# Six of eight sums of squares as two single-pass products of split squares, in a fused attention and expert kernel

## The chip, the cores and the metric

One core of one Trainium2 chip. The metric is the device time of one execution in microseconds (us), the median of several. The engines are named as the profile names them: PE is TensorE (matmuls; PEld its weight loads), DVE is VectorE, ACT is ScalarE, POOL is GpSimd, and SP is SyncE, which here only issues DMAs.

## What is computed

Causal attention with a bias from running sums gives 2304 rows of 512. Each row goes to one of eight experts, then through RMS normalization and a gated layer:

```python
for e in range(E):
    mask = expert_idx == e
    xe = x[mask]
    h = np.maximum(xe @ w1[e], 0.0)
    ye = h @ w2[e]
    out[mask] = gate_w[mask, None] * ye
...
rms = np.sqrt(np.mean(x * x, axis=-1, keepdims=True) + 1e-06)
xn = x / rms * rms_g
g = xn @ w_gate
silu = g * (1.0 / (1.0 + np.exp(-g)))
return (silu * (xn @ w_val)) @ w_out
```

The change concerns the mean of x*x, taken over the 512 features of each row that leaves an expert.

## The kernel before

The program runs attention, then the experts one after another, then the gated layer. In PE, ACT, DVE and SP each stage's instructions stand in the order in which the Python code emits them; each engine works its own list in that order and waits on semaphores for the others.

An expert s holds n rows, n from 312 down to 248 for experts 1 to 7 (`CAP`). Features lie on the partitions and rows in the columns. `gemm1` makes eight tiles f of the hidden layer, 24 products to a pair of tiles: every operand is split into a high part (rounded to `float32r`) and a low part (the rest), and a product is three `float32r` products (`PASSES`). After a tile ACT takes Relu (L918, `h`, high part) and DVE makes the low part (L919). `gemm2` makes four tiles c of the output: ACT copies each to `y` (L940) and squares it (L945), and DVE adds the squares up in `sq` (L946), so that `sq` holds, on each of the 128 partitions, the sum over four of the 512 features.

`finish(s)` sums `sq` over the partitions by one product of a 128x128 matrix of ones with `sq`, in plain `float32` (L960, tile `ms`), takes the root on ACT (L962), the reciprocal on DVE (L963) and scales `y` (L966). It stands one expert late, behind tile f = 1 of the next expert's `gemm1`, so that `sq` has been ready for a while. The six places at which this happens for experts 1 to 6 are called handovers 1 to 6 below; handover 1 lies in expert 2, and so on.

The weights of a later expert are loaded in pieces of 512 KB to `raw` (SP, L732, four staging buffers). `split` makes their parts: ACT casts the high part (L747), and DVE takes the rest one call later (L760). One `split` stands behind each of the four tiles of `gemm2` (two behind c = 1) and three stand in `gemm1`. The one behind c = 3 stands just ahead of Relu f = 0 of the next expert in ACT's list.

Of the kernel before, what the change touches and what calls it, by code (L numbers as in the profile page):

```python
# [7 lines left out]
F32 = mybir.dt.float32  # L8
F32R = mybir.dt.float32r
# [3 lines left out]
ALU = mybir.AluOpType  # L13
# [6 lines left out]
E = 8  # L20
# [4 lines left out]
CAP = (312, 304, 300, 292, 284, 268, 248)  # L25
CM = CAP[0]
# [33 lines left out]
def consts(k):  # L60
    nc, P = k.nc, k.cpool
    k.ident = P.tile([128, 128], F32, name="ident")
    nc.gpsimd.memset(k.ident, 0.0)
    nc.gpsimd.affine_select(out=k.ident, in_=k.ident, compare_op=ALU.not_equal, fill=1.0, base=0,
                            pattern=[[-1, 128]], channel_multiplier=1)
    k.w8 = P.tile([128, E], F32, name="w8")
    nc.gpsimd.iota(k.w8, pattern=[[-1, E]], base=E, channel_multiplier=0, allow_small_or_imprecise_dtypes=True)
    k.tid = P.tile([128, 5], F32, name="tid")
    nc.gpsimd.iota(k.tid, pattern=[[128, 5]], base=0, channel_multiplier=1, allow_small_or_imprecise_dtypes=True)
    k.w8v = P.tile([128, 5, E], F32, name="w8v")  # L70
    nc.gpsimd.tensor_copy(k.w8v, k.w8.unsqueeze(1).broadcast_to((128, 5, E)))
    nc.gpsimd.memset(k.w8v[64:128, 4, :], 0.0)
    k.base = P.tile([128, E], F32, name="base")
    nc.gpsimd.iota(k.base, pattern=[[REG, E]], base=0, channel_multiplier=0, allow_small_or_imprecise_dtypes=True)
    k.ereg = P.tile([1, E], F32, name="ereg")
    nc.gpsimd.iota(k.ereg, pattern=[[REG, E]], base=0, channel_multiplier=0, allow_small_or_imprecise_dtypes=True)
    k.eid = P.tile([1, E], F32, name="eid")
    nc.gpsimd.iota(k.eid, pattern=[[1, E]], base=0, channel_multiplier=0, allow_small_or_imprecise_dtypes=True)
    cap = P.tile([1, E], F32, name="cap")
    k.cap, k.na = cap[:, 0:RANKS], cap[:, RANKS:E]  # L80
    for n, c in enumerate(CAP):
        nc.gpsimd.memset(k.cap[:, n:n + 1], float(c))
    k.ones32 = P.tile([128, 128], F32, name="ones32")
    nc.gpsimd.memset(k.ones32, 1.0)
    eps = P.tile([128, 6], F32, name="eps6")
    k.eps6, k.gv = eps[:, 0:1], eps[:, 2:6]
    nc.vector.memset(k.eps6, 1e-6)
    nc.scalar.activation(eps[:, 1:2], k.eps6, AF.Exp)
    k.nb = P.tile([1, NB], U32, name="nb")
    P.tile([128, 32], F32, name="space")  # L90
# [727 lines left out]
def tiles_of(n):  # L818
    return tuple((t, min(128, n - 128 * t)) for t in range((n + 127) // 128))
# [17 lines left out]
def load_late(k):  # L837
    k.xl = y_tile(k, "xl")[:, 0:XROW].unsqueeze(1)
    load_rows(k, k.xl, 0, LATE, slice(NA, NA + LATE))
# [10 lines left out]
def ids(k, x, tiles):  # L850
    nc = k.nc
    row = k.rpool.tile([1, CM], F32, name=f"ids{k.uid()}", tag="ids", bufs=1)
    ps = k.psum.tile([128, 512], F32, name=f"ip{k.uid()}", tag="b")
    n = 0
    for t, m in tiles:
        nc.tensor.transpose(ps[0:1, n:n + m], x[0:m, t, DM:DM + 1], k.ident[0:m, 0:m])
        n += m
    row = row[:, 0:n]
    nc.scalar.copy(row, ps[0:1, 0:n])
    return row  # L860


def keep_ids(k, row, column):
    n = row.shape[-1]
    k.nc.sync.dma_start(out=k.tokd[bass.ds(column, n)].unsqueeze(0), in_=row)
# [88 lines left out]
    return number(k, OFF + piece, NTOK)  # L954


def finish(k, s, n):
    nc = k.nc
    ps = k.psum.tile([128, 512], F32, name=f"ms{s}", tag="b")
    nc.tensor.matmul(ps[:, 0:n], k.ones32, k.sq[s][:, 0:n], start=True, stop=True)  # L960
    r = k.sq[s][:, 0:n]
    nc.scalar.activation(r, ps[:, 0:n], AF.Sqrt, bias=k.eps6, scale=1.0 / DM)  # L962
    nc.vector.reciprocal(r, r)  # L963
    y = k.y[s][:, :, 0:n]
    for c in range(4):
        nc.vector.scalar_tensor_tensor(y[:, c, :], y[:, c, :], k.gv[:, c:c + 1], r, op0=ALU.mult, op1=ALU.mult)  # L966
    return y
# [33 lines left out]
def turn_rows(k, y, out):  # L1001
    nc = k.nc
    ps = k.psum.tile([128, 512], F32, name=f"yt{k.uid()}", tag="b")
    for c in range(4):
        nc.tensor.transpose(ps[:, 128 * c:128 * c + 128], y[:, 128 * c:128 * c + 128], k.ident)
    nc.vector.tensor_tensor(out, ps.rearrange("p (c n) -> p c n", c=4),
                            k.gv.unsqueeze(2).broadcast_to((128, 4, 128)), op=ALU.mult)
# [5 lines left out]
def moe(k, close):  # L1013
    k.y, k.sq = {}, {}

    def rank(n):
        for _ in range(n):
            next(k.last, None)

    k.order = [(s, u, q) for s in range(1, E) for u in range(4) for q in (0, 2)]  # L1020
    words = [(E, 2, f) for f in range(4 + EARLY_OUT, NF)] + [(E, 0, 0), (E, 1, 0)]
    for n, item in enumerate(words):
        k.order.insert(WORDS_AT + 9 * n, item)
    chain = iter(())
    row = ids(k, k.x[0], EARLY)
    keep_ids(k, row, 0)
    rank(RANK[0])
    for f in range(8):
        gemm1(k, 0, f, NA)
        rank(RANK[f + 1])  # L1030
        if f == 3:
            load_late(k)
        if f in (2, 4):
            split(k, 1, False)
        elif f == 5:
            rest(k)
    load_x(k, 1)
    feed(k, STG - 1)
    first = tiles_of(CAP[0])
    gemm2(k, 0, 0, NA)  # L1040
    rank(1)
    gemm2(k, 0, 1, NA)
    rank(1)
    gate(k, k.xl, ((0, 128),))
    gemm2(k, 0, 2, NA)
    xb = [k.rpool.tile([128, 4, CP], F32R, name=f"xb{n}", tag=f"xt{n}", bufs=1)[:, :, 0:128] for n in range(2)]
    turn_tile(k, k.xl[:, 0, :], *xb)
    row = ids(k, k.xl, ((0, 128),))
    keep_ids(k, row, column(k, 1))
    split(k)  # L1050
    gate(k, k.x[1], first)
    split(k)
    gemm2(k, 0, 3, NA)
    split(k)
    k.hr = y_tile(k, "hr")[:, 0:1024]
    rows_gemm1(k, xb, 0)
    split(k)
    rows_gemm1(k, xb, 1)
    hb = [k.mpool.tile([128, 8, CP], F32R, name=f"hb{n}", tag=f"h{n}")[:, :, 0:128] for n in range(2)]
    turn_tile(k, k.hr[:, 0:512], *[t[:, 0:4] for t in hb])  # L1060
    x_transpose(k, 1, (0, 1), first)
    turn_tile(k, k.hr[:, 512:1024], *[t[:, 4:8] for t in hb])
    x_transpose(k, 1, (2, 3), first)
    split(k)
    y = finish(k, 0, NA)
    row = ids(k, k.x[1], first)
    yr = k.hr.rearrange("p (a n) -> p a n", a=2)
    k.yr = yr[:, 0, :]
    rows_gemm2(k, hb)
    keep(k, y, NA, 0)  # L1070
    keep_ids(k, row, column(k, 2))
    split(k)
    head = iter(())
    for s in range(1, E):
        last = s == E - 1
        n = CAP[s - 1]
        if last:
            rest(k)
            close()
            glu_first(k)  # L1080
            next(head)
        else:
            load_x(k, s + 1)
        for f in range(8):
            gemm1(k, s, f, n)
            if s == 1 and f == 0:
                y = yr[:, 1, :].rearrange("p (c n) -> p c n", c=4)
                turn_rows(k, k.yr, y)
            if s > 1 and f == 1:
                y = finish(k, s - 1, CAP[s - 2])  # L1090
            if f == 5:
                keep(k, y, CAP[s - 2] if s > 1 else LATE, column(k, s))
                if not last:
                    gate(k, k.x[s + 1], tiles_of(CAP[s]))
            if f in (1, 3, 5) or (s == 1 and f < 3):
                split(k)
            next(head, None)
        for c in range(4):
            gemm2(k, s, c, n)
            next(chain, None)  # L1100
            if c == 1:
                split(k)
            if not last:
                if c in (1, 2):
                    x_transpose(k, s + 1, (2 * c - 2, 2 * c - 1), tiles_of(CAP[s]))
                if c == 1:
                    row = ids(k, k.x[s + 1], tiles_of(CAP[s]))
                if c == 3:
                    keep_ids(k, row, column(k, s + 2))
            split(k)  # L1110
            if c == 0 and s <= len(words):
                chain = decode_words(k)
                next(chain)
            if s == E - 2 and c == 1:
                head = glu_head(k)
            next(head, None)
    assert not k.staged and not k.order

    def tail():
        keep(k, finish(k, E - 1, CAP[-1]), CAP[-1], column(k, E))  # L1120

    k.tail = tail
# [941 lines left out]
```

## Time and profile before

| what | value |
|---|---|
| median of 3 runs | 839.87 us (839.81 to 841.09) |
| the profiled execution's own time | 838.61 us |
| its span from first to last instruction | 836.9 us |
| PE busy | 816.7 us, 98% |
| PEld / DVE / ACT / POOL busy | 746.7 / 639.6 / 461.9 / 227.0 us |
| chain that ended last, PE's share | 92% |
| granted TensorE clock, mean | 0.994 |

The profiled execution is 1.3 us under the median of the runs, and 1.7 us of it lie outside the span. The experts 1 to 7 take from about 223 us to 416 us of the span.

### The profile page before, as it was taken

How to read it: one execution, taken by the hardware profiler on the slowest of the kernel's cores; microseconds unless marked ns; L12 is line 12 of the kernel's file. 1: busy time of each engine (PE TensorE's matmuls, PEld its weight loads, DVE VectorE, ACT ScalarE, POOL GpSimd, SP SyncE). 2: the span in 40 equal slices, each digit the busy share in tenths (PEclk: the TensorE clock that was granted, in tenths of full speed). 3: DMA queues.
4: the chain of work that ended last, by engine and by line, in shares of the span. 5: the costliest groups of instructions: out<-in, count | busy, mean ns of one | idle time of the engine just before them, and what ended most of it. 6: DMA issues, size and time to landing. Idle time of an engine off the chain costs nothing.

```text
span 836.9 us, 15788 instructions
## 1 busy us (share of the span) xinstructions
PE 816.7 (98%) x5622; PEld 746.7 (89%) x5622; DVE 639.6 (76%) x1425; ACT 461.9 (55%) x1060; POOL 227.0 (27%) x249
## 2 busy tenths in 40 slices
PE   7999999999999999999999999999999999999994
PEld 4777767789899999999999999999999998899994
DVE  6657688965866768777698988988888869868880
ACT  5988989865756656566543433333333334553440
POOL 3335856332000000000221233444343351031120
PEclk9999999999999999999999999999999999999997
DMA  7999989236567566767661332322222376344510
GB/s 226 299 320 314 315 245 295 84 126 214 193 193 245 179 228 204 237 206 233 225 197 66 131 109 103 131 94 98 104 100 99 108 282 191 81 151 146 159 52 29
DMA packets 79757, 146.72 MB, mean 175 GB/s; under 512 B 7424, under 2 KB 44315, under 8 KB 79667
## 3 DMA queue, kind: packets, MB, share of 16 engines
q1 hardware_dynamic: 76707, 136.08, 51.4%
q0 software_dynamic: 2912, 9.46, 3.0%
q8 instruction: 46, 0.75, 0.4%
q14 instruction: 44, 0.36, 0.1%
q10 hardware_dynamic: 48, 0.07, 0.0%
HBM read 108.04 MB, written 37.54 MB: 174 GB/s over the span
## 4 chain that ended last, share of the span: by engine, by line
PE 92%; DVE 3%; ACT 2%; DMA 1%; issue 1%; SPq 0%; POOL 0%; POOLq 0%; DVEq 0%; ACTq 0%
PE gg L1320 29%; PE g L938 12%; PE g L915 12%; PE gp L1778 10%; PE go L1713 6%; PE pvy L419 5%; PE t L373 5%; PE s L310 5%; PE tl L447 2%; PE sm L341 1%; PE xp L886 1%; ACT pt L406 1%; DMA ringa<-ytd 1%; PE r L987 1%; PE r L976 1%
## 5 line engine op out<-in xcount | busy, mean ns | idle before, releaser
L938 PE MATMUL g<-h,u 128*128 128x256 f32 (+7 forms) x768 | 104.3, 294 | 0.0
L915 PE MATMUL g<-xt,u 128*128 128x256 f32 (+7 forms) x768 | 103.9, 294 | 0.0
L915 PEld LDWEIGHTS g<-xt,u 128*128 128x128 f32 x768 | 101.0, 188 | 0.8
L938 PEld LDWEIGHTS g<-h,u 128*128 128x128 f32 x768 | 100.5, 188 | 0.5
L1297 POOL TENSOR_TENSOR ws<-raw,ws 128x512 fp32r<-128x512 f32 (+1 forms) x25 | 33.0, 1335 | 219.4 <-ACT ws L1292 219.4
L747 ACT CAST u<-raw 128x1024 fp32r<-128x1024 f32 x62 | 65.1, 1050 | 20.9 <-DMA raw<-in_w 20.9
L354 ACT ACTIVATE p<-sc,nm 128x128 f32<-128x128 f32 (+3 forms) x128 | 71.2, 581 | 6.0 <-DVE nm L298 6.0
L760 DVE TENSOR_TENSOR u<-raw,u 128x1024 fp32r<-128x1024 f32 x58 | 70.3, 1216 | 0.9 <-ACT u L747 0.9
L1320 PE MATMUL gg<-gx2a,ws 128*128 128x384 f32 x360 | 67.4, 335 | 0.6 <-DVE tmp L1342 0.6
L1320 PE MATMUL gg<-gx0a,ws 128*128 128x384 f32 x360 | 67.7, 336 | 0.0
L1320 PE MATMUL gg<-gx1a,ws 128*128 128x384 f32 x360 | 67.1, 335 | 0.0
L1320 PEld LDWEIGHTS gg<-gx2a,ws 128*128 128x128 f32 x360 | 62.8, 188 | 0.9 <-DVE tmp L1342 0.9
L1320 PEld LDWEIGHTS gg<-gx0a,ws 128*128 128x128 f32 x360 | 63.1, 188 | 0.0
L1320 PEld LDWEIGHTS gg<-gx1a,ws 128*128 128x128 f32 x360 | 62.7, 188 | 0.0
L1358 POOL TENSOR_TENSOR hs<-tmp,hs 128x384 f32<-128x384 f32 x27 | 30.3, 1122 | 106.2 <-ACT hs L1356 106.2
L406 ACT COPY pt<-t 128x512 f32<-128x512 f32 (+3 forms) x160 | 56.0, 451 | 3.0 <-PE t L373 2.0
L373 PE MATMUL t<-ident,p 128*128 128x128 f32 x400 | 52.1, 275 | 0.1
L373 PEld LDWEIGHTS t<-ident,p 128*128 128x128 f32 x400 | 44.5, 140 | 8.5 <-DVE nm L298 8.3
L1699 POOL DMA_INDIRECT out<-raw,oid x18 | 20.5, 1138 | 112.1 <-DVE raw L1800 64.5
L419 PE MATMUL pvy<-pt,vp 128*64 128x512 f32 (+4 forms) x320 | 47.5, 428 | 0.9 <-ACT pt L406 0.9
L1338 ACT COPY tmp<-gg 128x384 f32<-128x384 f32 x27 | 13.0, 482 | 57.1 <-PE gg L1320 55.4
L1248 ACT ACTIVATE raw<-raw 128x512 f32<-128x512 f32 x31 | 21.1, 681 | 36.0 <-DVE raw L1246 35.8
(391 smaller groups left out, 1809.5 us busy)
## 6 DMA issues: line engine op xcount, KB each, us to landing
raw<-in_w SPq DMA_DIRECT2D x64, 512.0 KB
hd<-hs SPq DMA_DIRECT2D x72, 192.0 KB
xs<-zrow SPq DMA_DIRECT2D x8, 771.0 KB
raw<-in_wo SPq DMA_DIRECT2D x12, 512.0 KB
raw<-in_wg SPq DMA_DIRECT2D x12, 512.0 KB
raw<-in_wv SPq DMA_DIRECT2D x12, 512.0 KB
vp<-in_v SPq DMA_DIRECT2D x16, 320.0 KB
in<-cumd SPq DMA_DIRECT2D x20, 256.0 KB
```

The source lines that it names most:

```text
L310: k.nc.tensor.matmul(ps[h], st.q[r, 128 * i:128 * i + 128], st.k[r, 0:w], start=True, stop=p >= BYPE)
L354: k.nc.scalar.activation(out, st.s[i, h][:, 0:w], AF.Exp, bias=st.nm[:, n:n + 1], scale=-1.0, accum_out=acc)
L373: nc.tensor.transpose(ps[:, off:off + 128], src[:, 128 * j:128 * j + 128], k.ident)
L406: nc.scalar.copy(b, a)
L419: nc.tensor.matmul(st.y[r, a - 64:512], st.v[:, h, j, :], k.pt[:, h, o:o + S - a], start=j == 0, stop=j == 4)
L747: nc.scalar.copy(w[:, :, 0, :], raw)
L760: k.nc.vector.tensor_tensor(w[:, :, 1, :], raw, w[:, :, 0, :].bitcast(F32), op=ALU.subtract)
L915: nc.tensor.matmul(ps[:, 0:n], w[:, f % 4, a, 128 * kc:128 * kc + 128], x[b][:, kc, 0:n], start=kc == 0 and i == 0, stop=kc == 3 and i == 2)
L938: nc.tensor.matmul(ps[:, 0:n], w[:, f % 4, a, 128 * c:128 * c + 128], k.h[b][:, f, 0:n], start=f == 0 and i == 0, stop=f == 7 and i == 2)
L1320: k.nc.tensor.matmul(k.ps[u, bank], w[:, a, 128 * c:128 * c + 128], x[:, b, GT * c:GT * c + GT], start=first and c == 0 and n == 0, stop=c ...
L1713: k.nc.tensor.matmul(k.acc[tau], c[:, a, 128 * t:128 * t + 128], w[:, b, :], start=f == 0 and i == 0, stop=f == NF - 1 and i == 2)
L1778: k.nc.tensor.matmul(k.acc[i, bank], t[:, a, j, :], item_weight(k, j, w, b), start=first and j == 0 and n == 0, stop=j == 5 and n == 2, sk ...
```

## The change

For experts 1 to 6 `sq` is split like every other operand: ACT casts a high part and DVE subtracts it to get a low part, in a new function called behind tile f = 0 of the next expert's `gemm1`. Behind tile f = 1 the sum is then two `float32r` products that add up in one bank, high part first. Experts 0 and 7 keep the `float32` product. The ones become a `float32r` tile, which POOL makes out of the identity.

```diff
@@ consts
-    k.ones32 = P.tile([128, 128], F32, name="ones32")
-    nc.gpsimd.memset(k.ones32, 1.0)
+    k.ones32 = P.tile([128, 128], F32R, name="ones32")
+    nc.gpsimd.tensor_scalar(k.ones32, k.ident, 0.0, 1.0, op0=ALU.mult, op1=ALU.add)
@@ new function, and finish
+def square_parts(k, s, n):
+    t = k.mpool.tile([128, 4, CM], F32R, name=f"sp{s}", tag="y", bufs=2)
+    hi, lo = k.parts = t[:, 0, 0:n], t[:, 1, 0:n]
+    k.nc.scalar.copy(hi, k.sq[s][:, 0:n])
+    k.nc.vector.tensor_tensor(lo, k.sq[s][:, 0:n], hi.bitcast(F32), op=ALU.subtract)
+
+
 def finish(k, s, n):
     nc = k.nc
     ps = k.psum.tile([128, 512], F32, name=f"ms{s}", tag="b")
-    nc.tensor.matmul(ps[:, 0:n], k.ones32, k.sq[s][:, 0:n], start=True, stop=True)
+    if s in (0, E - 1):
+        nc.tensor.matmul(ps[:, 0:n], k.ones32.bitcast(F32), k.sq[s][:, 0:n], start=True, stop=True)
+    else:
+        for i, part in enumerate(k.parts):
+            nc.tensor.matmul(ps[:, 0:n], k.ones32, part, start=i == 0, stop=i == 1)
@@ moe, in the loop over f of gemm1
             if s == 1 and f == 0:
                 y = yr[:, 1, :].rearrange("p (c n) -> p c n", c=4)
                 turn_rows(k, k.yr, y)
+            if s > 1 and f == 0:
+                square_parts(k, s - 1, CAP[s - 2])
             if s > 1 and f == 1:
                 y = finish(k, s - 1, CAP[s - 2])
```

The list of TensorE at handover 2 before the change (`ms` is the sum, `ones_96` the ones, `g_1` and `g_2` the tiles f = 1 and f = 2 of the next expert; what a row waits for stands in brackets):

```order
L915 MATMUL g_1_3912<-xt_3785,u_3599 128x300
L915 MATMUL g_1_3912<-xt_3784,u_3599 128x300
L960 MATMUL ms_3927<-sq_3711,ones_96 128x304 [waits DVE_49]
L915 MATMUL g_2_3940<-xt_3784,u_3599 128x300
L915 MATMUL g_2_3940<-xt_3785,u_3599 128x300
```

And with the change:

```order
L915 MATMUL g_1_3919<-xt_3789,u_3603 128x300
L915 MATMUL g_1_3919<-xt_3788,u_3603 128x300
L971 MATMUL ms_3934<-sp_3916,ones_96 128x304 [waits Activation_49]
L971 MATMUL ms_3934<-sp_3916,ones_96 128x304 [waits DVE_49]
L915 MATMUL g_2_3948<-xt_3788,u_3603 128x300
L915 MATMUL g_2_3948<-xt_3789,u_3603 128x300
```

One product that waited for VectorE's last add has become two: the first waits for ScalarE's cast and the second for VectorE's subtraction.

VectorE's list at the same place with the change (`sp` holds the two parts; `h` the hidden layer's low parts of f = 0 and f = 1; `u` the weights' low parts):

```order
L946 TENSOR_TENSOR sq_3715<-sq_3715 128x304 [waits Activation_49]
L760 TENSOR_TENSOR u_3855<-raw_3782,u_3855 128x2x512 [waits DMAHW1_49]
L919 SCALAR_TENSOR_TENSOR h_3900<-g_0_3901,h_3899 128x300 [waits Activation_49]
L961 TENSOR_TENSOR sp_3916<-sq_3715,sp_3916 128x304 [waits DMAHW5_49,Activation_49]
L919 SCALAR_TENSOR_TENSOR h_3900<-g_1_3919,h_3899 128x300 [waits Activation_49]
```

The subtraction (L961) is the only new row; it stands behind the low part of f = 0 and so behind ScalarE's Relu of f = 0, for which that row waits.

ScalarE's list there, with the change:

```order
L940 COPY y_3714<-g_3_3860 128x304 [waits PE_49]
L945 ACTIVATE sq_3715<-g_3_3860 128x304 [waits DVE_49]
L747 CAST u_3855<-raw_3786 128x2x512 [waits DMAHW2_49]
L918 ACTIVATE h_3899<-g_0_3901 128x300 [waits PE_49]
L960 CAST sp_3916<-sq_3715 128x304 [waits DMAHW5_49,DVE_49]
L918 ACTIVATE h_3899<-g_1_3919 128x300 [waits PE_49]
```

The cast to `sp` (L960 of the changed file) is the only new row; ahead of it stand the Relu of f = 0 and the cast of a weight piece, which waits for the piece's DMA. The parts take a buffer of the pool of `y`, and the wait for an earlier DMA out of that buffer (DMAHW5 here) goes from the first copy to the next `y` to this cast. SP's list is the same row for row.

## Rows read from the trace of the kernel before

**Rows 1.** Windows view: span, busy of PE, PEld, DVE, ACT, POOL; clock, DMA.

```profile
225.00:396.00 171.00, 171.00 (x1269) 166.83 (x1268) 124.69 (x189) 107.17 (x207) 0.63 (x1) 1.00 0.69 219
```

**Rows 2.** Chain of waits, 190 to 420: start us, us, what.

```profile
222.93 0.04 issue
...
251.51 3.31 PE g L915 x24
254.82 0.53 PE ms L960 x2
...
280.81 3.32 PE g L915 x24
284.13 0.51 PE ms L960 x2
...
313.21 0.51 PE ms L960 x2
...
341.22 0.49 PE ms L960 x2
...
368.84 0.48 PE ms L960 x2
...
391.08 2.72 PE g L915 x24
393.80 0.45 PE ms L960 x2
```

**Rows 3.** Waits of ACT, 225 to 395: us in total, times, longest.

```profile
ACT u L747 <- DMA raw<-in_w: 20.5, 13, 2.6
```

**Rows 4.** Timeline of ACT in expert 2 and at handover 2: start us, us, what.

```profile
268.71 0.41 ACT L940 COPY y<-g 128x304 f32<-128x304 f32 x1 [2.85 <-PE g L938]
...
283.54 1.05 ACT L747 CAST u<-raw 128x1024 fp32r<-128x1024 f32 x1 [1.43 <-DMA raw<-in_w]
284.49 0.73 ACT L918 ACTIVATE h<-g 128x300 fp32r<-128x300 f32 x2
```

**Rows 5.** Groups by form, 190 to 420: busy us, mean ns of one.

```profile
L915 PE MATMUL g<-xt,u 128*128 128x300 f32 x96 | 13.8, 303 | 0.0
L1292 ACT CAST ws<-raw 128x256 fp32r<-128x256 f32 x4 | 1.4, 410 | 0.0
L946 DVE TENSOR_TENSOR sq<-sq 128x304 f32<-128x304 f32 x3 | 1.4, 475 | 5.9 <-ACT sq L945 5.9
L1292 ACT CAST ws<-raw 128x512 fp32r<-128x512 f32 x2 | 1.3, 634 | 0.0
```

**Rows 6.** Timeline of DVE at handovers 1 to 6.

```profile
254.48 0.47 DVE L919 SCALAR_TENSOR_TENSOR h<-g,h 128x304 fp32r<-128x304 f32 x1
...
284.94 0.85 DVE L919 SCALAR_TENSOR_TENSOR h<-g,h 128x300 fp32r<-128x300 f32 x2 [1.19 <-ACT h L918]
...
314.04 0.47 DVE L919 SCALAR_TENSOR_TENSOR h<-g,h 128x292 fp32r<-128x292 f32 x1 [1.15 <-ACT h L918]
...
342.05 0.45 DVE L919 SCALAR_TENSOR_TENSOR h<-g,h 128x284 fp32r<-128x284 f32 x1 [1.07 <-ACT h L918]
...
370.18 0.44 DVE L919 SCALAR_TENSOR_TENSOR h<-g,h 128x268 fp32r<-128x268 f32 x1 [1.32 <-ACT h L918]
...
392.18 2.35 DVE L760 TENSOR_TENSOR u<-raw,u 128x1024 fp32r<-128x1024 f32 x2
394.45 0.41 DVE L919 SCALAR_TENSOR_TENSOR h<-g,h 128x248 fp32r<-128x248 f32 x1
```

**Rows 7.** Timeline of PE in the gated layer, and its group on the page.

```profile
493.11 0.44 PE L1320 MATMUL gg<-gx0b,ws 128*128 128x384 f32 x1 [0.17 <-DVE tmp L1340]
...
L1320 PE MATMUL gg<-gx0a,ws 128*128 128x384 f32 x360 | 67.7, 336 | 0.0
```

**Rows 8.** Timeline of POOL at the start of the program.

```profile
6.67 0.45 POOL L284 TENSOR_TENSOR p<-in,half 128x128 f32<-128x128 f32 x1 [0.92 <-DMA in<-in_q]
```

**Rows 9.** Timeline of SP between handovers 1 and 2.

```profile
276.10 4.15 SPq L732 DMA_DIRECT2D raw<-in_w  x4
```

## The prediction

> **What bounds the kernel now.** I read the windows first. From 225 to 396 us, the stretch in which the change does its work, TensorE is busy for all 171.00 us, while VectorE has 124.69 and ScalarE 107.17, and the granted clock is 1.00, the upper level (2.4 GHz) [rows 1]. So what TensorE saves or waits here moves the end by as much, unless a later wait takes it back. The chain of waits confirms it: it runs through TensorE alone, and each handover's sum appears in it as a piece of two instructions, 0.53 us for the first (312 columns) down to 0.45 us for the sixth (268 columns) [rows 2]. The reader should see that these pieces are all that the old product costs: 2.97 us over the six.
>
> Then I asked whether the other engines are ready when TensorE comes to the sum, since the new products wait for work that the old one did not need. They are not ahead. ScalarE waited 13 times for a weight piece, 20.5 us in all [rows 3]. At handover 2 such a wait ends at 283.54 with a cast of 1.05 us, and behind it the Relu of f = 0 starts only at 284.49 [rows 4], although TensorE has by then finished f = 1 too, at 284.13 [rows 2]. Nobody on TensorE waited for that Relu until `gemm2`, so this lateness was free. The change puts a TensorE instruction behind it.
>
> **The change, part by part.** *Product, without waits.* A `float32r` product of nearly the same width takes 3.31/24 = 0.138 us in the tiles ahead of handover 1 and 2.72/24 = 0.113 us ahead of handover 6 [rows 2]. Two of them cost 0.28 to 0.23 us, about 1.51 us over the six handovers against 2.97 us. By itself this is a gain of about 1.46 us.
>
> *Cast of the high part.* Two Relus in a row take 0.73 us [rows 4] at 0.42 each, so an instruction starts 0.31 us behind the one before. The cast thus starts at 284.49 + 0.31 = 284.80. Its length at 304 columns lies between 0.410 us at 256 and 0.634 us at 512 for a cast out of SBUF [rows 5]; by a straight line it is 0.45. It ends at about 285.25. If nothing overlaps, it ends at 285.35. TensorE's first product can then start, and is itself some 1.1 us late.
>
> *Subtraction of the low part.* VectorE's row ahead of it, the low part of f = 0, starts at 284.94; two such rows take 0.85 us at 0.47 each [rows 6], so the next may start 0.38 us behind the first, at 285.32. By then the cast is done. The price of the subtraction is that of the add of squares of the same width, 0.475 us [rows 5]: it ends at 285.80.
>
> *Second product.* The nearest row for the step from another engine's end to TensorE's start is 0.04 us, the issue piece ahead of a product (0.05 taken here) [rows 2]. A product takes 303 ns from start to end [rows 5], and the one that started behind a wait took 0.44 us where the mean of its kind is 0.336 [rows 7], 0.11 more. The second product ends at 285.80 + 0.05 + 0.41 = 286.26. The old one ended at 284.13 + 0.51 = 284.64 [rows 2]. Handover 2 costs 1.62 us instead of saving 0.25.
>
> *The other five, by the same sum* (VectorE's start of the low part of f = 0 [rows 6], + 0.38, + 0.48 to 0.44 for the width, + 0.46, against the end of the old piece [rows 2]): handover 1: 255.80 against 255.35, +0.45; 3: 315.35 against 313.72, +1.63; 4: 343.35 against 341.71, +1.64; 5: 371.48 against 369.32, +2.16; 6: 395.73 against 394.25, +1.48. At the sixth it is not a DMA that makes VectorE late: two rests of weights in a row, 2.35 us from 392.18, stand ahead [rows 6]. All six together: +8.98 us, the saving already counted in. If the weight load is not exposed behind the wait, 0.11 goes off each (8.3); if the cast does not overlap the Relu, some 0.06 to 0.1 is added at five of them (9.4). I take 9.0.
>
> *Is each stall paid anew?* TensorE's wait lets the others catch up, so the next lateness might shrink. I think it does not. By tile c = 0 of expert 2 ScalarE had caught up on its own: it idled 2.85 us until TensorE [rows 4]. What makes it late again comes after that: four pieces are issued in one burst of 4.15 us from 276.10 [rows 9], when VectorE's work behind c = 1 has freed the buffers, and this shifts with TensorE. A stall moves the whole pattern to the right.
>
> *What costs nothing.* The `float32r` ones are made at the start, where GpSimd soon idles 0.92 us until a DMA [rows 8]; they are first needed some 200 us later. ScalarE's six casts (some 0.3 us each in its list) and VectorE's six subtractions (0.38) fall into engines with 64 and 46 us idle in this stretch [rows 1]; without that cover, on the chain, they would be some 4 us, and the part that is on the chain stands in the sums above. The wait for a DMA that moves to the cast is for a store issued nearly an expert earlier. Behind the subtraction VectorE's low part of f = 1 is queued, then the reciprocal and the scaling of `y`, which feed the store at f = 5; all of them now start from a sum that is late by the same time as TensorE itself. Behind the cast, Relu f = 1 is pushed 0.3 us; TensorE needs it only in `gemm2`.
>
> **The rivals.** *A: the sums are just cheaper* (this one ends on the other side). If the low part were there when f = 1 ends, each handover would save half: 839.87 - 1.46 = 838.4 us. It decides from the point at which the subtraction ends by 284.13 at handover 2 instead of 285.80: the Relu would have to be 1.7 us earlier, so the weight pieces would have to land 1.7 us earlier. Nothing in the change does that, and the wait of 1.43 us in [rows 4] speaks against it. The Trainium skill's page FP8 and Floating Point Precision (TensorE Precision Notes) says that a true FP32 product takes four passes and reduced precision is read in one; by this rule alone two products would take half the time of one, and the change would gain. The pieces in [rows 2] agree on the ratio; the rule leaves out when the parts are there.
>
> *B: only part is paid.* If a stall brought the weight pieces forward against TensorE, handovers 1 and 2 would pay in full (2.1 us) and the later four about half (3.4 us): 845.4 us.
>
> *C: lateness grows.* The rests and loads that queue behind the subtraction come 0.38 us later, the pieces land later, and the next Relu is later still; with some 0.6 us more at each of five handovers it is +12: 851.9 us. Against it: ScalarE's idle 2.85 us absorbs more than that.
>
> *D: the clock drops.* If TensorE's granted clock fell to the lower level (1.2 GHz) at each stall and a pair of tiles (3.3 us) ran at it, six times 3.3 us would come on top: about 869 us. In this stretch the clock is 1.00 throughout [rows 1], but no stall of 2 us stands in it. The Trainium skill's page TensorE: Matmul & The Clock Gate (Why this matters for your kernels) warns that longer idle gaps between matmul bursts bring half rate; no row of this trace shows one in mid-kernel.
>
> **How the numbers follow.** The sum is made on the profiled execution, 838.61 us by its own time, 1.26 under the median of the runs; I add it to the median: 839.87 + 9.0 = 848.9 us. Chances: forecast (8 to 10 us more) 0.70; B 0.15; C 0.08; A 0.05; D 0.02. The likeliest case has a range of its own, 847.9 to 849.9, and the overall range reaches down into B and up towards C: 844.5 to 851.0. A change under 0.2% (1.7 us) can hardly be told from none here. Faster is A, 0.05; the same is the tail of B, 0.04; slower is the rest, 0.91.
>
> **What would show it.** In the profile after, the two products of each handover should stand apart, the second waiting for VectorE, with TensorE idle 0.4 us at handover 1 and 1.5 to 2.1 us at the others; the chain of waits should leave TensorE there and go through VectorE's subtraction, ScalarE's Relu or cast, the weight cast and a DMA. TensorE's busy time should not grow. I would be wrong if the second product started within 0.1 us of the first, or if ScalarE's wait for weight pieces shrank by what TensorE loses.

## The result, and the profile after

The changed kernel takes 849.22 us (median of 4 runs, 848.67 to 850.99) against 840.48 us for the kernel before beside it: a ratio of 1.0108, interval 1.0089 to 1.0126. That is 8.7 us more, where 9.0 was forecast. Measured once more on another chip (below) the ratio was 1.0100.

The first thing to read is who TensorE waits for. In the kernel before it waited for nobody in the experts [rows 1]. These are the waits of TensorE in the changed kernel, 225 to 430 us (total, times, longest):

```profile
PE ms L971 <- ACT sp L960: 6.2, 5, 1.7
PE ms L971 <- DVE sp L961: 1.5, 2, 1.3
```

The windows answer to [rows 1] over the same stretch:

```profile
225.00:396.00 171.00, 164.10 (x1185) 158.36 (x1184) 118.28 (x181) 101.92 (x196) 0.00 (x0) 0.99 0.66 208
```

TensorE, busy for all 171 us before, is now idle for 6.9 us of the same length (handover 6 lies behind it). Why it is idle stands in the timeline of handover 2 of the changed kernel (start, duration, what; in brackets the idle time before and what ended it):

```profile
285.55 1.05 ACT L747 CAST u<-raw 128x1024 fp32r<-128x1024 f32 x1 [1.70 <-DMA raw<-in_w]
...
286.50 0.41 ACT L918 ACTIVATE h<-g 128x300 fp32r<-128x300 f32 x1
286.81 0.43 ACT L960 CAST sp<-sq 128x304 fp32r<-128x304 f32 x1
286.95 0.47 DVE L919 SCALAR_TENSOR_TENSOR h<-g,h 128x300 fp32r<-128x300 f32 x1 [1.45 <-ACT h L918]
...
287.30 0.96 PE L971 MATMUL ms<-sp,ones 128*128 128x304 f32 x2 [1.38 <-ACT sp L960]
287.33 0.47 DVE L961 TENSOR_TENSOR sp<-sq,sp 128x304 fp32r<-128x304 f32 x1
```

The Relu stands behind a weight cast that waited 1.70 us for its DMA; the cast of the high part follows the Relu by 0.31 us, the subtraction follows the low part of f = 0 by 0.38 us, and the second product follows the subtraction. The chain of waits, which ran through TensorE alone before, leaves it at this place and ends at the weight piece's DMA:

```profile
279.29 6.24 DMA raw<-in_w
285.53 0.02 issue
285.55 0.03 ACT u L747
285.57 0.93 issue
286.50 0.42 ACT h L918
286.92 0.02 issue
286.95 0.03 DVE h L919
286.98 0.35 issue
287.33 0.48 DVE sp L961
287.81 0.04 issue
287.85 0.41 PE ms L971
288.26 9.95 PE g L915 x72
```

At handover 6 no DMA stands in the chain. The subtraction comes late behind VectorE's own work, the second of two rests of weights and the low part of f = 0:

```profile
404.43 1.22 DVE u L760
405.65 0.33 DVE h L919
405.97 0.36 DVE sp L961
...
406.37 0.39 PE ms L971
```

The chain also shows what each handover costs: the start of the row behind the last product, against the end of the old piece in [rows 2].

```profile
224.07 0.65 PE yt L1016 x4
...
257.13 10.03 PE g L915 x72
...
318.97 9.52 PE g L915 x72
...
349.09 9.38 PE g L915 x72
...
378.86 10.45 PE g L915 x72
...
406.76 8.16 PE g L915 x72
```

Ahead of the experts this execution was already 1.10 us later than the profiled one of before (224.07 against 222.97, where expert 1 begins): attention, which the change leaves alone. Counting from there, the handovers cost 0.68, 1.84, 1.64, 2.12, 2.16 and, less the next item, 1.46 us: 9.90 us. The 72 products behind handover 5 took 10.45 us, 1.51 more than the 8.94 that they take at the upper clock; the clock is the reason (below). 9.90 + 1.51 + 1.10 = 12.51 us, and the span is 12.4 us longer (849.3 against 836.9). The profiled execution is the slowest of the four; the median lies near to where the handovers alone put it (838.61 + 9.9 = 848.5).

Of the signs that the prediction named, most came. At handover 2 the second product started 0.55 us behind the first (287.30 and 287.85), and ScalarE's wait for weight pieces did not shrink: 21.7 us over the stretch of [rows 3], where it was 20.5. One did not come: TensorE's busy time grew, from 816.7 to 821.3 us. Of these 4.6 us, 1.1 go with the later start of the experts, and 3.2 lie between the start of expert 1 and the gated layer (190.48 and 193.69 us of TensorE's time): 1.5 are the clock's, and the other 1.7 fit the products themselves, a pair of which took 0.92 to 0.96 us behind a wait at handovers 2 to 5, where the old piece took 0.48 to 0.51 [rows 2].

### The profile page after: what moved, and what is told of

Its sections match the earlier page's. It is cut to its first block, busy times and chain, and to the rows that moved or that the text cites. A ratio compares the mean times of both kernels' runs of the same rounds, so it can differ in the third digit from the quotient of the medians.

```text
span 849.3 us, 15802 instructions
## 1 busy us (share of the span) xinstructions
PE 821.3 (97%) x5622; PEld 748.5 (88%) x5622; DVE 643.8 (76%) x1431; ACT 464.1 (55%) x1066; POOL 227.7 (27%) x249
## 4 chain that ended last, share of the span: by engine, by line
PE 80%; DMA 9%; DVE 5%; ACT 2%; issue 2%; POOL 0%; SPq 0%; POOLq 0%; DVEq 0%; ACTq 0%
PE gg L1333 29%; PE gp L1791 10%; PE g L938 10%; PE g L915 10%; PE go L1726 6%; DMA raw<-in_w 5%; PE s L310 3%; PE pvy L419 3%; PE t L373 3%; DMA in<-cumd 2%; PE tl L447 1%; PE sm L341 1%; DMA in<-in_q 1%; PE xp L886 1%; DMA ringa<-ytd 1%
## 5 line engine op out<-in xcount | busy, mean ns | idle before, releaser
L747 ACT CAST u<-raw 128x1024 fp32r<-128x1024 f32 x62 | 65.0, 1048 | 21.7 <-DMA raw<-in_w 21.7
L1712 POOL DMA_INDIRECT out<-raw,oid x18 | 20.5, 1137 | 112.0 <-DVE raw L1813 64.5
```

Of the source, the lines that this page charges most:

```text
L747: nc.scalar.copy(w[:, :, 0, :], raw)
```

## The experiments

The theory is that of the prediction: the products themselves save a little, and TensorE waits because the parts stand behind a weight cast that waits for DMA (handovers 1 to 5) or behind rests of weights on VectorE (6). Rivals: the extra work on ScalarE and VectorE costs the time; the subtraction alone is what is late; the parts are fine anywhere but the products are slow. Edits are shown against the changed kernel. The first four kernels ran on one chip (before: 839.26 us, median of 28). Three more ran on a second (before: 845.71 us, median of 23): five early parts, the later sum and the changed kernel once more. The repeat of the later sum ran on a third. The three profiles from the second chip reach expert 1 at 228.8 to 230.8 us, all others at 222.6 to 224.4, so much of its longer time arises ahead of the experts.

**Both parts made, nothing waits for them.**

```diff
-    if s in (0, E - 1):
+    if True:
         nc.tensor.matmul(ps[:, 0:n], k.ones32.bitcast(F32), k.sq[s][:, 0:n], start=True, stop=True)
```

> Both parts are made as in the changed kernel, but the sum is the float32 product of the squares as before, so that nothing waits for the parts. Theory: ScalarE's and VectorE's extra work is covered; 840 to 841, as before. Rival (the extra work in their lists, the later loads and rests, cost the time): 845 to 849.

840.95 us, ratio 1.0014 (1.0004 to 1.0024): 1.2 us by the ratio, 1.7 between the medians. The extra work is not the cause of 8.7 us, but it is not quite free either. The place that the trace shows is in expert 7, in the timeline of TensorE of this kernel:

```profile
406.40 0.38 PE L938 MATMUL g<-h,u 128*128 128x248 f32 x1 [0.38 <-DVE h L919]
```

TensorE waits 0.38 us for the low part of the last hidden tile. The work that VectorE and ScalarE hand to each other through expert 7 has no slack, so the sixth subtraction comes out at its end: VectorE idles there twice, 0.67 and 0.46 us, for a Relu of ScalarE, in this kernel as in the kernel before. From the end of handover 6 to the end of the seventh sum this kernel loses 0.63 us on the kernel before; at handovers 1 to 6 it loses nothing.

**The low part left out of the sum.**

```diff
-        for i, part in enumerate(k.parts):
-            nc.tensor.matmul(ps[:, 0:n], k.ones32, part, start=i == 0, stop=i == 1)
+        nc.tensor.matmul(ps[:, 0:n], k.ones32, k.parts[0], start=True, stop=True)
```

> The low part is made, but left out of the sum, which is one product of the high part. Theory: TensorE waits for ScalarE alone; the wait ends 0.55 us earlier at handovers 2 to 5, and one product falls away; by the prediction's rows the end of the sum moves by +1.1, +1.1, +1.1 and +1.6 us at handovers 2 to 5 and by -0.2 at 1 and 6: +4.4 us, about 844.7. Rival (the subtraction on VectorE is what TensorE waits for in the main): at most 1 us over before, 841.5.

844.11 us, ratio 1.0047 (1.0032 to 1.0062): 3.9 us more by the ratio and 4.9 between the medians, where the theory had 4.4 and the rival at most 1. (The expectation's times count from 840.3 us, 1 us above this chip's kernel before.) The waits of TensorE in this kernel:

```profile
PE ms L970 <- ACT sp L960: 4.5, 4, 1.9
PE g L938 <- DVE h L919: 0.7, 1, 0.7
```

So about half of the loss is ScalarE's lateness, with no subtraction in the way at all. The other half goes with the low part: at handover 2 of the changed kernel the second product starts 0.55 us behind the first, and at the sixth handover VectorE is the late one. Without the low part there is no wait at handovers 1 and 6.

**The weight cast moved behind the high part**, at handovers 2 to 5.

```diff
             if s > 1 and f == 0:
                 square_parts(k, s - 1, CAP[s - 2])
+                if 2 < s < E - 1:
+                    split(k)
...
-            split(k)
+            if c < 3 or s in (1, E - 2, E - 1):
+                split(k)
             if c == 0 and s <= len(words):
```

> The changed kernel, but the weight cast behind c = 3 goes behind the cast of the high part, at handovers 2 to 5 only. Theory: Relu f = 0 then starts when TensorE ends f = 0, the parts are ready before f = 1 ends, and these four handovers no longer wait; handovers 1 and 6 keep their 0.5 and 1.5 us: 841 to 842. Rival (the rests and loads that come later now are late for something else, or the wait comes from the subtraction's place in VectorE's list): 845 or more.

840.75 us, ratio 1.0019 (1.0008 to 1.0029): most of the changed kernel's loss is gone, but for the two handovers left as they were (0.25 and 1.41 us in the trace). ScalarE and TensorE of this kernel at handover 2:

```profile
283.14 0.42 ACT L918 ACTIVATE h<-g 128x300 fp32r<-128x300 f32 x1 [0.50 <-PE g L915]
283.46 0.44 ACT L960 CAST sp<-sq 128x304 fp32r<-128x304 f32 x1
...
284.61 0.44 PE L971 MATMUL ms<-sp,ones 128*128 128x304 f32 x2
```

Now ScalarE waits for TensorE ahead of the Relu, not the other way round, and both products follow each other without a wait. Handovers 2, 3 and 4 gain 0.23, 0.20 and 0.10 us, and handover 5 loses 0.11, because its second product still waits a little for VectorE. The edit moves the whole `split`, and so VectorE's rest of the piece before as well; but that rest was not in the way, since VectorE idled 1.45 us for the Relu at handover 2 of the changed kernel (above). The place of one weight cast in ScalarE's list decides: this is the cause of handovers 2 to 5, shown.

**The parts made early**, right behind c = 3 of `gemm2`.

```diff
-            if s > 1 and f == 0:
-                square_parts(k, s - 1, CAP[s - 2])
...
             gemm2(k, s, c, n)
+            if c == 3 and not last:
+                square_parts(k, s, n)
             next(chain, None)
```

> The parts are made right behind tile c = 3 of gemm2, ahead of the weight cast, instead of behind tile f = 0 of the next expert. Theory (the products are late because ScalarE's Relu, and with it the cast and the subtraction, stand behind a weight cast that waits for a DMA): VectorE's last add ends at about 282.6 at handover 2, the subtraction at about 283.5, TensorE comes at 284.1 and waits for nothing. All six handovers save what two products cost less than one, 1.4 us against the kernel before: about 839.0 where before is 840.5. Rival (making or multiplying the parts is itself what costs): it stays near the changed kernel, 847 to 849.

839.56 us, ratio 1.0004 (0.9995 to 1.0013): the loss is gone, but the gain of 1.4 us that the theory named did not come. TensorE waits at no handover, 1 and 6 among them. The chain of this kernel at handovers 1 and 5, and the one place where its TensorE waits:

```profile
255.74 0.29 PE ms L971 x2
...
368.99 0.31 PE ms L971 x2
```

```profile
405.15 0.38 PE L938 MATMUL g<-h,u 128*128 128x248 f32 x1 [0.76 <-DVE h L919]
```

At the first the piece is about half of its old length, as forecast; at the fifth it is a little longer, the parts being just ready. Together handovers 1 to 6 gain 1.1 us. Expert 7 then takes 0.88 us of that back: there the subtraction and VectorE's wait for the cast stand ahead of the weights' rests, and all of VectorE's list behind them comes 0.93 us later, counted from the last add of squares, up to the last low part.

**The same for experts 1 to 5 only**; the sixth sum stays `float32`. The edit is shown against the version with six early parts.

```diff
-    if s in (0, E - 1):
+    if s in (0, E - 2, E - 1):
...
-            if c == 3 and not last:
+            if c == 3 and s < E - 2:
```

> The kernel whose parts are made right behind c = 3, but for experts 1 to 5 alone; the sum of expert 6 is the float32 product again. Theory: the five handovers save the 0.24, 0.23, 0.20, 0.23 and 0.03 us that the trace of the version with six shows, VectorE's list in expert 7 is as before and TensorE's wait of 0.8 us there is gone: 0.9 us under before (0.9989). Rival (the 0.8 us in expert 7 has another cause than the sixth subtraction): as before or slower.

844.79 us against 845.71, ratio 0.9992 (0.998 to 1.0005): in the right place, but not told from no change. Its trace confirms half of the expectation: there is no wait in expert 7. But it also shows that early parts are not safe. ScalarE at its handover 5:

```profile
371.20 1.05 ACT L747 CAST u<-raw 128x1024 fp32r<-128x1024 f32 x1 [3.01 <-DMA raw<-in_w]
...
373.37 0.43 ACT L960 CAST sp<-sq 128x284 fp32r<-128x284 f32 x1 [0.52 <-DVE sq L946]
```

The copy of c = 3 stands behind another weight cast, the one of c = 2. It waited 3.01 us this time, the parts came late after all, and this handover cost 0.35 us.

**The sum moved later**, behind f = 3, with the parts where the change puts them.

```diff
-            if s > 1 and f == 1:
+            if s > 1 and f == 3:
                 y = finish(k, s - 1, CAP[s - 2])
```

> The changed kernel, parts behind f = 0, but the two products and what follows them stand behind tile f = 3 instead of f = 1. Theory: the parts are then there, no product waits, and handovers save 0.2 us each; in expert 7 VectorE has the subtraction more and TensorE waits up to 0.8 us: 0.3 to 1 us under before. Rival (the root, the reciprocal, the scaling and the store of y come too late behind f = 3): 1 us or more over before.

843.54 us against 845.71, ratio 0.9975 (0.9961 to 0.9989). That is 2.2 us between the medians, and 0.9 to 3.3 us by the interval; its trace gains 1.23 us between the start of expert 1 and the gated layer, and nothing behind. So it was run again.

> The version with the sums behind f = 3 again, beside the kernel before on another day's chip. Its trace showed six handovers that save 0.17 to 0.22 us each, 1.23 us in all, and no wait of TensorE in the experts. Theory (that is all there is to gain): 1.2 us under before, 0.9985. Rival (the 0.9975 measured first is real, and more than the products is saved somewhere): 2 us or more under before.

838.41 us against 839.60, ratio 0.9988 (0.9979 to 0.9997): 1.2 us, the theory's number. The chain of this run has no wait in the experts, and the six sums stand as one piece each, 0.29, 0.28, 0.27, 0.27, 0.26 and 0.25 us; the first and the last:

```profile
257.94 0.29 PE ms L971 x2
...
395.32 0.25 PE ms L971 x2
```

The handovers gain 0.17 to 0.23 us each over the two profiles of this version. The intervals of its two measurements overlap. The sixth subtraction does not show in expert 7 here. That the sum's move also eases VectorE's list there (root, reciprocal and scaling come behind two more low parts) fits, but was not tried by itself. This version is faster than both kernels, than the one before by little more than 0.1%.

**The changed kernel once more**, for the spread of its waits and its clock.

> The changed kernel once more, for its clock. Theory: the lateness comes from DMA landings, so each handover's wait differs by up to 1 us from one execution to the next, the sum staying at 9 to 10 us; in some executions the clock falls to its lower level behind one of the longest waits, and these are 1 to 1.7 us longer with a mean clock of 0.992 instead of 0.994 to 0.996. Rival (the clock has nothing to do with it): the times do not go with the clock.

853.71 us against 845.71, ratio 1.0100 (1.0077 to 1.0123). The chain behind its six handovers:

```profile
230.80 0.66 PE yt L1016 x4
...
264.11 10.03 PE g L915 x72
...
294.37 9.94 PE g L915 x72
...
325.14 9.52 PE g L915 x72
...
354.37 9.39 PE g L915 x72
...
383.30 8.94 PE g L915 x72
...
409.65 8.16 PE g L915 x72
```

Its stage before the experts is 7.8 us longer than in the first profile of before; from there the handovers cost 0.94, 0.97, 1.70, 1.23, 1.32 and 1.42 us, 7.58 us in all against 9.90 in the first execution. The waits that hang on a DMA differ by up to 0.9 us between the two executions; the sixth, which hangs on VectorE, by 0.04. So the theory's "9 to 10 us" was too narrow. The mean clocks of its six runs were 0.995 for four, 0.993 for the fifth (854.2 us) and 0.990 for the longest (858.5 us): longer runs go with a lower clock. In the profiled one, the 854.2 us, the clock fell at 138 to 141 us, in attention, which the change leaves alone.

## Why the prediction was right

*Product, without waits.* Right in kind, a little large. Without waits a pair of products takes 0.29 to 0.25 us, 1.62 us for six against 2.97 in [rows 2], 1.35 less; over the whole of the experts TensorE gains 1.2 us by it, forecast 1.46.

*Cast, subtraction, second product.* Right in each term. The cast took 433 ns at 304 columns (0.45 forecast), the subtraction 467 (475 forecast), the steps between were 0.31 and 0.38 us as read from [rows 4, 6], TensorE started 0.04 us behind the subtraction and the product behind a wait took 0.41 us. The extra 0.11 us fell on both products of a handover, not on the second alone; only the second lies at the end of the sum, so the time forecast did not suffer, but the sign that TensorE's busy time would not grow failed.

*The six together.* 9.0 forecast; 9.90 and 7.58 in two profiles, 8.7 and 8.0 between the medians. The single handovers were off by up to 0.8 us, because each took the landing times of one execution as fixed. They are not: in the first profile the six came out 0.9 us above the forecast, in the second 1.4 us below. The mechanism and the size were right; that the medians came within 0.3 and 1.0 us is in part luck.

*Is each stall paid anew?* Yes. From the start of tile f = 0 to its Relu pass 3.8 and 3.2 us on the mean of handovers 1 to 5 in the two profiles of the changed kernel. In kernels whose TensorE does not wait there it is 3.6 (before), 3.5 (parts made and unused), 3.2 and 3.0 us (the later sum, twice): the waits do not make ScalarE's lateness smaller or larger beyond what executions differ by. The later handovers cost no less than the earlier ones. So rivals B and C fall. That a burst of pieces makes ScalarE late anew each time fits, but was not tried by itself.

*What costs nothing.* Wrong at one place, by 0.4 to 0.8 us: the sixth subtraction has no cover in expert 7, as the three kernels show that make it, sum behind f = 1 and do not wait at handover 6 (0.38, 0.72 and 0.76 us). In the changed kernel itself this is hidden by the 1.4 us that TensorE already waits there. The sum over a stretch of 171 us was the wrong view for it; the idle time that counts is that of expert 7 alone.

*Rival A* was a true mechanism with its condition unmet: moving a weight cast behind the parts, making the parts earlier or taking the sum later each gives the gain of about 0.2 us at most of the handovers concerned; only the later sum gave it at all six. *Rival D*, the clock: seen in one of two profiles of the changed kernel, once instead of six times, at 1.5 us instead of 3.3 (half of the 3.2 us or so that ran at the lower level).

## What to carry to other kernels

Before putting a new dependence on the engine that bounds the kernel, read when the other engines are at that place of their lists, not how busy they are: here ScalarE had a third of the stretch idle, and at four of six handovers its part still came 1.2 to 1.75 us behind TensorE in one profile and 0.5 to 1.1 in another. Such lateness cost nothing as long as nothing waited for it. Price a halved instruction together with the chain that feeds it; 0.2 us was saved at a handover, and the wait for Relu, cast and subtraction that came on the path cost 1.2 us and more at most of them. If the parts are needed, leave them where they are and move the consumer until the chain is done in the worst of several profiles; here two profiles of the later sum show no wait, while making the parts earlier went wrong once.

## What the runs showed of the hardware

*Landing times differ by about a microsecond between executions of the same loads*. At handover 2, where a cast of a piece waits for its DMA, the DMA's part of the chain is 6.24 us in the first profile of the changed kernel and 5.36 in the second; it begins 3.2 us ahead of tile f = 0 in both. The second profile's row:

```profile
286.26 5.36 DMA raw<-in_w
```

The Relu of f = 0 started 4.06 and 3.18 us behind the start of its tile, and the handover cost 1.84 and 0.97 us. Terms of a sum that end in a DMA deserve a range from more than one trace.

*TensorE's clock fell to its lower level for about 3.4 us in mid-kernel*, in some executions only. In the first profile of the changed kernel it did so behind handover 5 (windows: span, busy of PE, PEld, DVE, ACT, POOL, clock, DMA):

```profile
378.00:379.00 1.00, 0.88 (x5) 0.67 (x6) 0.76 (x3) 0.29 (x2) 0.00 (x0) 1.00 0.74 184
379.20:382.40 3.20, 3.20 (x16) 3.20 (x15) 2.94 (x4) 1.52 (x3) 0.00 (x0) 0.50 0.68 232
383.00:389.00 6.00, 6.00 (x50) 6.00 (x50) 5.06 (x8) 4.36 (x8) 0.00 (x0) 1.00 0.50 124
```

TensorE had waited 1.7 us just before and was busy again when the clock fell to 0.50 (1.2 GHz). The kernel with the high part alone did the same behind its wait of 1.9 us at handover 5. But in the first profile of the kernel with the later sum, which has no wait in the experts, the clock was at 0.50 in attention:

```profile
137.50:140.80 3.30, 3.30 (x18) 3.29 (x17) 2.37 (x12) 2.23 (x6) 3.19 (x5) 0.50 1.03 393
```

There too TensorE had waited a little earlier, as it had in the second profile of the changed kernel, whose clock fell at 137.8. The timelines of TensorE in these two and in the kernel with five early parts:

```profile
136.34 0.91 PE L310 MATMUL s<-in 64*128 64x384 f32 x2 [1.09 <-ACT vp L431]
136.15 0.91 PE L310 MATMUL s<-in 64*128 64x384 f32 x2 [1.13 <-ACT vp L431]
136.72 0.91 PE L310 MATMUL s<-in 64*128 64x384 f32 x2 [1.10 <-ACT vp L431]
```

All four falls in mid-kernel came 1.1 to 1.7 us after TensorE had resumed from a wait of 1.09 to 1.94 us. Yet such a wait does not always bring one: in the third kernel here the clock stayed at 1.00, as it did behind the 1.67 us at handover 4 of the changed kernel. So the waits of the change may bring a fall, at 1.5 us each time, but it also comes ahead of the experts, where the change does nothing, and whether the change makes it more frequent stays open.
